# Seven products in the last dense chunk, and expert weight sums kept as plain sums

## The chip, the cores and the metric

The kernel runs on one core of a Trainium2 chip. The metric is the device time of one execution in microseconds; the times before are 1785.57, 1784.61 and 1784.65 us, median 1784.65.

PE is the matmul engine, PEld its weight load, DVE the vector engine, ACT the scalar engine, POOL the general one; SP issues transfers. A tile lies in SBUF (on-chip memory, 128 partitions) or in PSUM (the banks that PE writes to).

## The reference

All in float32. Attention with 32 packed rows, for 4 batches, 8 heads, 576 positions and head width 64:

```python
p_packed = sm_attn(p, k, v)
out = sm_attn(q, p_packed, p_packed)
```

Its result becomes x, of 2304 tokens by 512, and goes through a dense layer and a layer of 8 experts that every token visits:

```python
h = x @ w_in                       # w_in 512 x 2048
g = h * (1.0 / (1.0 + np.exp(-h)))
x = g @ w_out                      # w_out 2048 x 512

logits = x @ w_gate
P = np.exp(logits - logits.max())
for _ in range(8):
    P /= P.sum(1, keepdims=True) + 1e-09
    P /= P.sum(0, keepdims=True) + 1e-09
    P *= N / E
for e in range(E):
    h = np.maximum(x @ w1[e], 0.0)     # w1[e] 512 x 1024
    out += P[:, e:e + 1] * (h @ w2[e]) # w2[e] 1024 x 512
```

## The kernel before

Every float32 operand of a large product is kept as a sum of two halves, hi (ACT casts it to the reduced type float32r) and lo (DVE subtracts hi from the raw value; `split`, lines 145 and 146). A product is three matmuls: hi by hi, hi by lo, lo by hi.

**Dense layer.** The hidden columns go in four chunks c of 512. Attention gives, for each batch, a small matrix U (its packed values times w_in) from which the hidden values come by 24 matmuls of 128x288 for half a batch and half a chunk (`gemm1`, line 652). U is made as Uh (ACT, line 637) and Ul (DVE, line 638). ACT applies silu from PSUM (683) and casts the hi half (684), DVE subtracts for the lo half (685); both halves lie in `ring`. The second product (`gemm2_wide`, line 736) takes tiles of 384 tokens by 128 output columns: 12 matmuls each, with d counting the four blocks of 128 output columns, and a token tile holding two thirds of a batch. A chunk has 24 such tiles, 288 matmuls. In half of the tiles the old x2 (the output so far) is copied into the PSUM bank first (`seed`) and ACT copies the sum back (741); in the others DVE adds (743).

**What runs beside it.** Two trickles of work are fed in as the dense chunks run, each by a counter that the products advance (`pump`): `convs(c + 1)`, which turns the raw w_in and w_out of the next chunk into rounded halves (lines 528 to 546, tiles `win`, `ct`), at rate `CONV`; and `pre_w1`, at rate `RATE[c]`, which prepares expert weights. The instruction order on PE, DVE and ACT is the order of the code here (a manual schedule).

**Expert weights.** A step s is one expert and one half of its 1024 hidden columns, 16 steps, each run for three groups of tokens: a small group (256 tokens, steps 0 to 15, plain products) and two large ones (steps 16 to 47) in which a product of 2 x 2 blocks is made from seven block products in place of eight (numbers 1 to 7). For these, four sums of blocks of w1 are needed in each step (products 6, 7, 5, 3), the products 1, 2 and 4 use plain blocks. `pre_w1` makes the four sums for all 16 steps (line 851, tiles `S`), splits each into halves (`po`) and SP stores both halves in device memory (`w1d<-po`). In the large groups `w1_get` fetches hi and lo (512 KB) for the products with sums, and for the others loads the raw block of 256 KB (`rb`) and splits it. In the small group w1 and w2 are loaded again and split into whole halves (`w1l`, `w2l`, 128x1024).

## Time and profile before

| what | value |
|---|---|
| profiled execution | 1784.47 us, span 1782.7 us, granted clock 1.0 |
| PE busy | 1764.3 us, 99% |
| DVE busy | 1438.8 us, 81% |
| ACT busy | 1066.4 us, 60% |
| POOL busy | 1.0 us, 0% |
| DMA queue q1 | 340.14 MB, 54.7% of 16 engines |
| dense layer's second product, line 736, on the chain | 8% |
| dense layer's first product, line 652, on the chain | 5% |
| large groups, lines 1153 and 1201, on the chain | PE d 34%, X 20%, Z 10%, Y 5% |
| small group, lines 1046 and 1065, on the chain | u 5%, d 4% |

The span is the stretch from the first to the last instruction in the trace, the profiled execution's time is 1.8 us more. The shares on the chain say which line's work was the last to end at each moment. A duration in the trace holds the time that an instruction takes from start to end; neighbours on one engine overlap, so that the distance of two starts in a full queue is shorter than the duration.

### The profile page before, as it was taken

To read this page: it belongs to the slowest core of one execution; us is meant where nothing else is said; L and a number is where in the kernel's file an instruction comes from. 1 tells how busy PE (TensorE), PEld (TensorE's weight loads), DVE (VectorE), ACT (ScalarE), POOL (GpSimd) and SP (SyncE) were. 2 spreads that over 40 slices of the span, in tenths; PEclk is the share of its full clock that TensorE was granted. 3 is DMA by queue.
4 is the path that set the end of the run, shared out by engine and by line. 5 is a ranking of instruction groups with operands and counts; after the bars stand their busy time and mean duration, and the time that the engine had idled before them with its cause. 6 is when DMAs were issued, how large, how long until landed. Compare 5 with 4: busy or idle time off the path is not lost.

```text
span 1782.7 us, 25352 instructions
## 1 busy us (share of the span) xinstructions
PE 1764.3 (99%) x9564; PEld 1506.0 (84%) x9564; DVE 1438.8 (81%) x1918; ACT 1066.4 (60%) x1694; POOL 1.0 (0%) x8
## 2 busy tenths in 40 slices
PE   7999999999999999999999999999999999999998
PEld 4999999989998888888888888888888888888887
DVE  7868796759676988999889999887777777777778
ACT  6776675644454666665666666656555555555555
POOL 0000000000000000000000000000000000000000
PEclk9999999999999999999999999999999999999999
DMA  9326676875664655465544455964454444445432
GB/s 353 139 95 214 245 263 249 329 258 172 221 209 161 229 181 183 160 203 187 197 163 171 172 187 195 324 221 166 156 174 164 155 154 148 170 155 171 148 130 94
DMA packets 141498, 341.75 MB, mean 192 GB/s; under 512 B 11952, under 2 KB 49472, under 8 KB 140480
## 3 DMA queue, kind: packets, MB, share of 16 engines
q1 hardware_dynamic: 141376, 340.14, 54.7%
q8 instruction: 75, 1.23, 0.3%
q14 instruction: 47, 0.39, 0.1%
HBM read 256.66 MB, written 83.44 MB: 191 GB/s over the span
## 4 chain that ended last, share of the span: by engine, by line
PE 95%; DVE 2%; DMA 2%; ACT 1%; issue 0%; SPq 0%; DVEq 0%; ACTq 0%
PE d L1153 34%; PE X L1201 20%; PE Z L1201 10%; PE g2w L736 8%; PE g L652 5%; PE Y L1201 5%; PE u L1046 5%; PE d L1065 4%; PE g L704 3%; DMA v<-in_v_dram 1%; PE u L251 1%; DMA kq<-in_kT_dram 0%; PE pp L367 0%; PE s L251 0%; PE lg L1235 0%
## 5 line engine op out<-in xcount | busy, mean ns | idle before, releaser
L146 DVE TENSOR_TENSOR lo<-hb,hi 128x1024 fp32r<-128x1024 f32 x224 | 273.5, 1221 | 33.4 <-ACT hi L145 32.3
L1153 PE MATMUL d<-hi,w2f 128*128 128x512 f32 x896 | 294.2, 389 | 0.0
L1201 PE MATMUL X<-xf,w1l 128*128 128x512 f32 x1152 | 276.9, 389 | 0.0
L145 ACT CAST hi<-hb 128x1024 fp32r<-128x1024 f32 x224 | 235.4, 1052 | 64.9 <-PE d L1153 59.6
L1201 PEld LDWEIGHTS X<-xf,w1l 128*128 128x128 f32 x1152 | 216.2, 188 | 44.9
L1161 ACT COPY M<-d 128x512 f32<-128x512 f32 x234 | 137.4, 589 | 143.9 <-PE d L1153 140.7
L1165 DVE TENSOR_TENSOR M<-d,M 128x512 f32<-128x512 f32 x204 | 140.1, 687 | 100.8 <-PE d L1153 100.8
L1153 PEld LDWEIGHTS d<-hi,w2f 128*128 128x128 f32 x896 | 168.1, 188 | 34.9
L1153 PE MATMUL d<-lo,w2f 128*128 128x512 f32 x448 | 174.3, 389 | 0.0
L1153 PE MATMUL d<-hi,w2l 128*128 128x512 f32 x512 | 167.8, 389 | 0.0
L736 PE MATMUL g2w<-ring,woh 128*128 128x384 f32 x576 | 147.6, 337 | 0.0
L1149 ACT COPY d<-M 128x512 f32<-128x512 f32 x216 | 127.1, 589 | 21.1 <-DVE M L1165 19.7
L1153 PE MATMUL d<-hi,w2g 128*128 128x512 f32 x384 | 125.7, 389 | 0.0
L1153 PEld LDWEIGHTS d<-hi,w2l 128*128 128x128 f32 x512 | 96.1, 188 | 20.3 <-ACT d L1149 0.4
L736 PEld LDWEIGHTS g2w<-ring,woh 128*128 128x128 f32 x576 | 102.9, 188 | 8.6 <-issue 7.5
L1208 ACT COPY cp<-X 128x512 f32<-128x512 f32 x128 | 74.7, 583 | 47.2 <-PE X L1201 47.1
L1153 PE MATMUL d<-lo,w2l 128*128 128x512 f32 x256 | 99.6, 389 | 0.0
L1153 PEld LDWEIGHTS d<-lo,w2f 128*128 128x128 f32 x448 | 84.1, 188 | 17.5
L1201 PE MATMUL Y<-xf,w1f 128*128 128x512 f32 x384 | 97.3, 389 | 0.0
L736 PE MATMUL g2w<-ring,wol 128*128 128x384 f32 x288 | 96.3, 334 | 0.0
L1046 PE MATMUL u<-xs,w1h 128*128 128x256 f32 x512 | 94.4, 285 | 0.0
L145 ACT CAST w1f<-rb 128x512 fp32r<-128x512 f32 x96 | 59.8, 624 | 55.8 <-PE d L1153 41.0
(219 smaller groups left out, 3469.0 us busy)
## 6 DMA issues: line engine op xcount, KB each, us to landing
r<-in_moe_w_dram SPq DMA_DIRECT2D x128, 512.0 KB, 4.0
w1l<-w1d SPq DMA_DIRECT2D x128, 512.0 KB, 4.0
w1d<-po SPq DMA_DIRECT2D x64, 512.0 KB, 4.5
w2d<-w2f SPq DMA_DIRECT2D x64, 512.0 KB, 4.0
w2l<-w2d SPq DMA_DIRECT2D x64, 512.0 KB, 3.5
rb<-in_moe_w_dram SPq DMA_DIRECT2D x96, 256.0 KB, 2.6
sb<-in_moe_w_dram SPq DMA_DIRECT2D x48, 256.0 KB, 2.7
pb<-pd SPq DMA_DIRECT2D x16, 512.0 KB, 4.9
```

Of the source, the lines that this page charges most:

```text
L145: act.copy(out=hi, in_=raw)
L146: eng.tensor_tensor(out=lo, in0=raw, in1=hi.bitcast(F32), op=ALU.subtract)
L652: pe.matmul(ps, lhs[:, fs], rhs, start=(n == 0), stop=(n == 5))
L736: pe.matmul(ps[:, :TW], lhs[:, f % 2, ds], ring[f // 2][:, 2 * (f % 2) + rhs, q], start=(n == 0 and not on), stop=(n == 11), skip_group_ch ...
L1046: pe.matmul(ps[:, i], w[:, k % 2, f], x[:, k], start=(n == 0), stop=(n == 11))
L1065: pe.matmul(ps, h[:, l, f % 2, 128 * tt:128 * tt + 128], w[:, f % 2], start=(fh == 0 and n == 0), stop=(fh == 1 and n == 11))
L1149: act.copy(out=ps, in_=m)
L1153: pe.matmul(ps, w[:, l, c, 128 * d:128 * d + 128], r[:, c], start=(n == 0 and not seed), stop=(n == 5), skip_group_check=seed)
L1161: act.copy(out=m, in_=ps)
L1165: dve.tensor_tensor(m, ps, m, op=ALU.add)
L1201: pe.matmul(ps, w[:, l, c, 128 * i:128 * i + 128], x[:, r, c], start=(n == 0 and p in (1, 7)), stop=(n == 5), skip_group_check=p in (2, 6, ...
L1208: act.copy(out=t, in_=ps)
```

## The change

- In the last chunk (c = 3) the second product is made from seven block products: the hidden values as 2 x 2 blocks of 256 hidden columns and 288 tokens, w_out as 2 x 2 blocks of 256 by 256. The h-forms are differences of raw silu values (`minus`), split by ACT and DVE into `ft`; the weight forms `wS` are made from the converted raw w_out by four sums and seven splits (`w_forms`). The seven products of a batch accumulate in three pairs of PSUM banks, X (products 1, 6, 5, 3), Z (7, 4) and Y (2, which is seeded with x2); after each product DVE adds the bank's present value to one of the four x2 blocks, for Y ACT copies it. Each product is 2 blocks of output columns times 6 matmuls of 128x288.
- `pre_w1` writes the sums over their raw blocks, with two pairs of raw tiles (`r1`, `rx`), and POOL stores the two tiles of a step plainly (`keep_sums`); for the steps in `WHOLE` the sums are split and POOL stores hi and lo (`keep_form`). The steps in `LATER` get their sums in the small group, in the last two parts of the step before. The rates change; no such work is left in the last chunk.
- In the large groups a sum that is kept plain is loaded like a raw block (256 KB), ACT casts hi and writes minus hi into the lo half, and POOL issues a transfer that adds the stored sum to it. `rb` has three tiles for two and is loaded one part later.

The diff, cut to its core:

```diff
-RATE = {1: 36 / 64, 2: 36 / 64, 3: 41 / 53}
-CONV = 0.6
+RATE = {1: 23 / 64, 2: 23 / 64}
+CONV = {1: 0.6, 2: 0.8}
 TW = 384
 LATE = 3
 AHEAD = 3
+WHOLE = (0, 1, 15)
+LATER = (8, 10, 12, 14)
...
+            if c == NC - 1:
+                wz[j] = z.rearrange("p (k f) -> p k f", k=2)
+                return
...
+    SUM = {6: (0, 0), 7: (0, 1), 3: (1, 0), 5: (1, 1)}
+
+    def part(s, p):
+        j, h = SUM[p]
+        return raw1[s, j][:, :, 256 * h:256 * h + 256]
+
+    def sums_a(s):
+        dve.tensor_tensor(part(s, 5), part(s, 7), part(s, 5), op=ALU.add)
+        dve.tensor_tensor(part(s, 7), part(s, 6), part(s, 7), op=ALU.subtract)
+
+    def sums_b(s):
+        dve.tensor_tensor(part(s, 6), part(s, 5), part(s, 6), op=ALU.subtract)
+        dve.tensor_tensor(part(s, 3), part(s, 3), part(s, 6), op=ALU.subtract)
+
+    def keep_sums(s):
+        for j in range(2):
+            t = tc.dram_tile([128, 2, FH], F32, name=f"w1s{s}_{j}")
+            nc.gpsimd.dma_start(t, raw1[s, j])
+            for h in range(2):
+                w1d[s, {v: k for k, v in SUM.items()}[j, h]] = t[:, :, 256 * h:256 * h + 256]
+
+    def keep_form(s, p):
+        t = unit([128, 2, 2, 256], F32R, f"po{s}_{p}")
+        split(t[:, 0], t[:, 1], part(s, p))
+        nc.gpsimd.dma_start(dram(w1d, s, p), t.bitcast(F32))
+
+    def pre_w1(todo):
+
+        for i in range(2):
+            for j in range(2):
+                load_w1(todo[i], j, ("r1", "rx")[i])
+        yield
+        yield
+        later = None
+        for i, s in enumerate(todo):
+            sums_a(s)
+            if later:
+                load_w1(later[0], 0, later[1])
+                load_w1(later[0], 1, later[1])
+            yield
+            sums_b(s)
+            if s not in WHOLE:
+                keep_sums(s)
+            else:
+                for p in SUM:
+                    yield
+                    keep_form(s, p)
+            nxt = todo[i + 2] if i + 2 < len(todo) else 0 if i % 2 == 0 else None
+            later = None if nxt is None else (nxt, ("r1", "rx")[i % 2])
+            yield
+        if later:
+            load_w1(later[0], 0, later[1])
+            load_w1(later[0], 1, later[1])
 
...
         t = st[name].tile([128, 2, 256], F32, tag=name, name=f"rb{s}_{p}")
         r, c = 256 * (p != 1), FH * fh + 256 * (p == 4)
-        nc.sync.dma_start(t, w1[e, r:r + 256, c:c + 256].rearrange("(c p) f -> p c f", p=128))
+        nc.sync.dma_start(t, w1[e, r:r + 256, c:c + 256].rearrange("(c p) f -> p c f", p=128)
+                          if p in (1, 2, 4) else w1d[s % G0, p])
         raw1[s, p] = t
 
...
     def w1_get(s, p):
-        if p not in (1, 2, 4):
+        if s % G0 in WHOLE and p not in (1, 2, 4):
             wf[s, p] = get(w1d, s, p)
+            return
+        t = unit([128, 2, 2, 256], F32R, f"w1f{s}_{p}")
+        raw = raw1.pop((s, p))
+        if p in (1, 2, 4):
+            split(t[:, 0], t[:, 1], raw)
         else:
-            t = unit([128, 2, 2, 256], F32R, f"w1f{s}_{p}")
-            split(t[:, 0], t[:, 1], raw1.pop((s, p)))
-            wf[s, p] = t
+            act.copy(out=t[:, 0], in_=raw)
+            act.activation(t[:, 1], t[:, 0].bitcast(F32), AF.Copy, scale=-1.0)
+            nc.gpsimd.dma_start(t[:, 1], w1d[s % G0, p], accum_op=ALU.add)
+        wf[s, p] = t
 
     def w2_block(s, p):
...
-        for name, n in (("S", 4), ("r1", 2), ("po", 2)):
+        for name, n in (("S", 4), ("r1", 2), ("rx", 2)):
             open_(name, n, keep=name in ("S", "r1"))
-        box["pre"] = pre_w1(list(range(G0)), 0)
...
+    def w_forms():
+        while len(wz) < 2:
+            yield
...
+        ta, tb = (st["S"].tile([128, 2, 256], F32, tag="S", name=f"ws{n}") for n in "ab")
+
+        def form(p, x):
+            wS[p] = unit([128, 2, 2, 256], F32R, f"wS{p}")
+            split(wS[p][:, 0], wS[p][:, 1], x)
+
+        form(1, a11)
+        yield
+        dve.tensor_tensor(tb, a11, a21, op=ALU.subtract)
+        form(7, tb)
+        yield
+        dve.tensor_tensor(ta, a21, a22, op=ALU.add)
+        form(5, ta)
+        yield
...
+        yield
+
+    wf_ = w_forms()
...
+        def g_unit(k, j, half):
+            if k not in box["raw"]:
+                box["raw"][k] = dict(zip((11, 12, 21, 22, 5), raw_set(k)))
+            ps = box["pg"].tile([128, 2, 512], F32, tag="pg", name=f"g1_{k}{half}{j}")
+            for i in range(2):
+                gemm1_mm(ps[:, i, :HS], c, o[k], half, 2 * j + i)
+            act.activation(box["raw"][k][10 * (j + 1) + half + 1], ps[:, :, :HS], AF.Silu)
...
+        def h_form(k, p, x):
+            if "ft" not in box:
+                box["ft"] = hp.tile([128, 4, 2 * S], F32R, tag="h0", name="ft")
+            t = box["ft"][:, fn[0] % 4].rearrange("p (l c s) -> p l c s", l=2, c=2)
+            fn[0] += 1
+            split(t[:, 0], t[:, 1], x)
+            box["f"][k, p] = t
+
+        def minus(out_, a, b_):
+            dve.tensor_tensor(out_, a, b_, op=ALU.subtract)
+
+        def forms_a(k):
+            r = box["raw"][k]
+            h_form(k, 1, r[11])
+            minus(r[11], r[12], r[11])
+
+        def forms_b(k):
+            r = box["raw"][k]
+            minus(r[12], r[22], r[12])
+            h_form(k, 7, r[12])
+            minus(r[5], r[22], r[11])
+
+        def forms_c(k):
+            r = box["raw"][k]
+            h_form(k, 6, r[5])
+            minus(r[5], r[21], r[5])
...
+        CH = {1: "X", 6: "X", 5: "X", 3: "X", 7: "Z", 4: "Z", 2: "Y"}
+        OUT = {1: (0, 0), 6: (1, 0), 5: (1, 1), 3: (0, 1), 7: (1, 1), 4: (1, 0), 2: (0, 0)}
...
+        def seed2(k):
+            for d in range(2):
+                box["Y", d] = box["p3"].tile([128, 512], F32, tag="y", name=f"sY{k}{d}")
+                act.copy(out=box["Y", d][:, :HS], in_=acc_of(k, 2, d))
...
+        def product(k, p):
+            w, t, ch = wS[p], box["f"].pop((k, p)), CH[p]
+            for d in range(2):
+                if p in (1, 7):
+                    box[ch, d] = box["p3"].tile([128, 512], F32, tag="y", name=f"s{ch}{k}{d}")
+                ps = box[ch, d][:, :HS]
+                n = 0
+                for f in range(2):
+                    for l, r in ((0, 0), (0, 1), (1, 0)):
+                        pe.matmul(ps, w[:, l, f, 128 * d:128 * d + 128], t[:, r, f],
+                                  start=(n == 0 and p in (1, 7)), stop=(n == 5),
+                                  skip_group_check=p not in (1, 7))
+                        n += 1
+                dst = acc_of(k, p, d)
+                if p == 2:
+                    act.copy(out=dst, in_=ps)
+                else:
+                    dve.tensor_tensor(dst, ps, dst, op=ALU.add)
+            step()
...
+        need(4)
+        g_unit(0, 0, 0)
+        wide()
+        g_unit(0, 0, 1)
+        wide()
+        wide()
+        wide()
+        forms_a(0)
+        g_unit(0, 1, 1)
+        make_u(c, o[1])
+        forms_b(0)
+        g_unit(0, 1, 0)
+        for k in range(4):
+            r, more = box["raw"][k], k < 3
...
+            product(k, 1)
+            if k == 0:
+                forms_c(0)
+                need(5)
+                h_form(0, 4, r[5])
+            if more:
+                g_unit(k + 1, 0, 0)
+            h_form(k, 5, r[11])
+            product(k, 7)
+            h_form(k, 2, r[21])
+            need(6)
+            product(k, 6)
+            if more:
+                g_unit(k + 1, 0, 1)
+            h_form(k, 3, r[22])
+            need(7)
+            product(k, 4)
+            if more:
+                forms_a(k + 1)
+                g_unit(k + 1, 1, 1)
+            seed2(k)
+            product(k, 5)
+            if more:
+                forms_b(k + 1)
+                g_unit(k + 1, 1, 0)
+            if k < 2:
+                make_u(c, o[k + 2])
+            product(k, 2)
+            if k == 2:
+                cvn = pre0()
+            if more:
+                forms_c(k + 1)
+            product(k, 3)
+            if more:
+                h_form(k + 1, 4, box["raw"][k + 1][5])
+        for _ in cvn:
+            pass
...
-                q += 3
-                if q < 7 * NS and ORD[q % 7] in (1, 2, 4):
+                q += 2
+                if q < 7 * NS:
                     w1_block(q // 7, ORD[q % 7])
...
+                if s + 1 in LATER and slot >= 2:
+                    (sums_a, sums_b)[slot - 2](s + 1)
+                    if slot == 3:
+                        keep_sums(s + 1)
...
-        for name in ("acc", "r2", "gh", "po"):
...
+        for name in ("acc", "r2", "gh", "rx"):
             closers[name].close()
-        for name, n in (("hb", 6), ("hi", 3), ("lo", 3), ("rb", 2)):
+        for name, n in (("hb", 6), ("hi", 3), ("lo", 3), ("rb", 3)):
```

DVE at the place in chunk 2 where Ul of the third batch stands. `x2a` is the dense output, `po` and `S` the expert sums' halves and sums, `ring` the lo half of the hidden values, `ct` the raw w_out in conversion, `r` and `rx` raw expert blocks. Before:

```order
L743 TENSOR_TENSOR x2a_788<-g2w_2874,x2a_788 128x384
L146 TENSOR_TENSOR po_6_2891<-S_2_2832,po_6_2891 128x512
L685 TENSOR_TENSOR ring_103<-graw,ring_103 128x2x288
L531 TENSOR_SCALAR ct_2888<-ct_2888 128x1024
L532 TENSOR_SCALAR ct_2888<-ct_2888 128x1024
L146 TENSOR_TENSOR po_7_2915<-S_3_2849,po_7_2915 128x512
L685 TENSOR_TENSOR ring_1745<-graw,ring_1745 128x2x288
L534 SCALAR_TENSOR_TENSOR ct_2888<-rawout_2758,ct_2888 128x1024
L638 TENSOR_TENSOR Ul_2948<-u_2938,Uh_2947 128x1024
```


and after:

```order
L866 TENSOR_TENSOR r_71_2759<-r_70_2757,r_71_2759 128x2x256
L867 TENSOR_TENSOR r_70_2757<-r_70_2757 128x2x256
L748 TENSOR_TENSOR x2a_788<-g2w_2823,x2a_788 128x384
L533 TENSOR_SCALAR ct_2814<-ct_2814 128x1024
L534 TENSOR_SCALAR ct_2814<-ct_2814 128x1024
L870 TENSOR_TENSOR r_70_2757<-r_71_2759,r_70_2757 128x2x256
L871 TENSOR_TENSOR r_71_2759<-r_71_2759,r_70_2757 128x2x256
L690 TENSOR_TENSOR ring_103<-graw,ring_103 128x2x288
L536 SCALAR_TENSOR_TENSOR ct_2814<-rawout_2693,ct_2814 128x1024
L690 TENSOR_TENSOR ring_1747<-graw,ring_1747 128x2x288
L541 ISA ct_2814<-rawout_2693,ct_2814 128x2048
L643 TENSOR_TENSOR Ul_2891<-u_2881,Uh_2890 128x1024
```


Ul stands behind sums over raw blocks (lines 866 to 871) and three more conversion operations, in place of splits.

PE at the end of the dense layer, where the gate's logits `lg` follow (`g2w` is a bank of the second product, `woh` and `wol` the halves of w_out, `sX`, `sY`, `sZ` the banks of the seven products). Before:

```order
L736 MATMUL g2w_4379<-ring_1745,woh_3168 128x384 x2
L736 MATMUL g2w_4379<-ring_1745,wol_3169 128x384
L736 MATMUL g2w_4379<-ring_1745,woh_3168 128x384 x2
L736 MATMUL g2w_4379<-ring_1745,wol_3169 128x384
L1235 MATMUL lg_4402<-x2b_1369,wg 32x256 x3
L1235 MATMUL lg_4402<-x2b_1370,wg 32x256 x3
L1235 MATMUL lg_4402<-x2b_1371,wg 32x256 x3
```


and after, the last batch's seven products without the first two:

```order
L1542 MATMUL sX_4063<-ft,wS_3211 128x288 x6
L1542 MATMUL sX_4071<-ft,wS_3211 128x288 x6
L1542 MATMUL sZ_4085<-ft,wS_3480 128x288 x6
L1542 MATMUL sZ_4093<-ft,wS_3480 128x288 x6
L1542 MATMUL sX_4063<-ft,wS_3193 128x288 x6
L1542 MATMUL sX_4071<-ft,wS_3193 128x288 x6
L1542 MATMUL sY_4147<-ft,wS_3554 128x288 x6
L1542 MATMUL sY_4149<-ft,wS_3554 128x288 x6
L1542 MATMUL sX_4063<-ft,wS_3521 128x288 x6
L1542 MATMUL sX_4071<-ft,wS_3521 128x288 x6
L1267 MATMUL lg_4214<-x2b_1373,wg 32x256 x3
L1267 MATMUL lg_4214<-x2b_1374,wg 32x256 x3
```


Nothing of the first product lies between these, and each pair reads a form of `ft`.

ACT in a large group (`hb`, `hi` hidden values, `d` and `M` sums of products, `w1f` the halves of a w1 form, `w2f` those of w2). Before:

```order
L145 CAST xs_10402<-xr_9396 128x512
L145 CAST hi_2_10430<-hb_10177 128x1024
L145 CAST w1f_1_10427<-rb_1_10284 128x512
L1149 COPY d_10434<-M_6735 128x512
L1161 COPY M_6681<-d_10380 128x512
L145 CAST w2f_1_10451<-r_280_10208 128x512
L145 CAST w1f_2_10469<-rb_2_10332 128x512
L145 CAST hi_4_10473<-hb_10177 128x1024
```


and after:

```order
L948 CAST w1f_6_9842<-rb_6_9746 128x512
L949 ACTIVATE w1f_6_9842<-w1f_6_9842 128x512
L147 CAST w2f_7_9869<-S_3_9865 128x512
L1193 COPY M_6626<-d_9797 128x512
L1181 COPY d_9848<-M_6677 128x512
L948 CAST w1f_7_9898<-rb_7_9790 128x512
L147 CAST hi_3_9904<-hb_9731 128x1024
L949 ACTIVATE w1f_7_9898<-w1f_7_9898 128x512
L147 CAST w2f_5_9925<-S_1_9814 128x512
L1193 COPY M_6677<-d_9848 128x512
```


The rows of lines 948 and 949 are the hi half and minus hi of a sum, which ACT had no part in before.

## Rows read from the trace of the kernel before

**Rows 1.** The page: busy us, share of the span and instructions of each engine.

```profile
PE 1764.3 (99%) x9564; PEld 1506.0 (84%) x9564; DVE 1438.8 (81%) x1918; ACT 1066.4 (60%) x1694; POOL 1.0 (0%) x8
```

**Rows 2.** Chain that ended last, 340 to 376 us: start us, us, what.

```profile
...
345.95 8.32 PE g2w L736 x48
354.28 3.19 PE g L652 x24
...
369.96 4.44 PE lg L1235 x56
...
```

**Rows 3.** DVE's starts, 235.2 to 242.6 us: start, us, line, operation, out<-in.

```profile
235.49 0.55 DVE L743 TENSOR_TENSOR x2a<-g2w,x2a 128x384 f32<-128x384 f32 x1
235.96 0.68 DVE L146 TENSOR_TENSOR po<-S,po 128x512 fp32r<-128x512 f32 x1
236.55 0.75 DVE L685 TENSOR_TENSOR ring<-graw,ring 128x576 fp32r<-128x576 f32 x1
237.22 0.68 DVE L531 TENSOR_SCALAR ct<-ct 128x1024 f32<-128x1024 f32 x1
237.94 0.69 DVE L532 TENSOR_SCALAR ct<-ct 128x1024 uint32<-128x1024 uint32 x1
238.55 0.68 DVE L146 TENSOR_TENSOR po<-S,po 128x512 fp32r<-128x512 f32 x1
...
240.96 1.22 DVE L638 TENSOR_TENSOR Ul<-u,Uh 128x1024 fp32r<-128x1024 f32 x1
242.09 1.21 DVE L539 CUSTOM_DVE_ANT_0 ct<-rawout,ct 128x2048 uint16<-128x2048 uint16 x1
```

**Rows 4.** PE's starts from 241.9 us; in brackets the idle before and its releaser.

```profile
242.23 0.40 PE L652 MATMUL g<-a2h,Ul 128*128 128x288 f32 x1 [0.38 <-DVE Ul L638]
```

**Rows 5.** Lines by form, 131 to 400 us: count, busy us, mean ns, idle before.

```profile
L684 ACT CAST ring<-graw 128x576 fp32r<-128x576 f32 x48 | 32.4, 675 | 1.5
...
L637 ACT CAST Uh<-u 128x1024 fp32r<-128x1024 f32 x10 | 10.1, 1008 | 0.0
...
L741 ACT COPY x2a<-g2w 128x384 f32<-128x384 f32 x13 | 6.2, 480 | 11.5 <-PE g2w L736 11.4
```

**Rows 6.** Windows of chunk 1: length, busy us (instructions) of PE, PEld, DVE, ACT, POOL, ...

```profile
155.00:171.40 16.40, 16.24 (x113) 14.98 (x112) 14.11 (x21) 12.66 (x18) 0.00 (x0) 1.00 0.82 289
171.40:195.70 24.30, 24.30 (x164) 23.28 (x163) 23.30 (x34) 17.89 (x29) 0.00 (x0) 1.00 0.82 275
195.70:211.60 15.90, 15.90 (x113) 14.93 (x112) 10.13 (x16) 10.07 (x18) 0.00 (x0) 1.00 0.85 324
211.60:236.10 24.50, 24.50 (x161) 23.25 (x160) 20.55 (x30) 18.20 (x29) 0.00 (x0) 1.00 0.53 179
...
```

**Rows 7.** The page's DMA issues: count, KB each, median us from issue to landing.

```profile
r<-in_moe_w_dram SPq DMA_DIRECT2D x128, 512.0 KB, 4.0
...
w1d<-po SPq DMA_DIRECT2D x64, 512.0 KB, 4.5
...
rb<-in_moe_w_dram SPq DMA_DIRECT2D x96, 256.0 KB, 2.6
```

**Rows 8.** Windows of DVE alone, steps 7, 11 and 13 of the small group.

```profile
451.40:462.60 11.20, 6.41 (x9) 1.00 0.82 243
...
496.40:507.60 11.20, 9.16 (x12) 1.00 0.56 190
...
518.80:530.10 11.30, 8.49 (x10) 1.00 0.83 267
```

**Rows 9.** A weight block in a large group: ACT's cast, PE's first use, a window.

```profile
899.05 0.62 ACT L145 CAST w1f<-rb 128x512 fp32r<-128x512 f32 x1 [0.60 <-PE d L1153]
...
920.61 0.62 PE L1201 MATMUL X<-xf,w1f 128*128 128x512 f32 x2
...
640.00:1110.00 470.00, 470.00 (x2075) 389.19 (x2074) 423.80 (x566) 296.65 (x467) 0.00 (x0) 1.00 0.52 182
```

More of the change, by code (lines that the diff above doesn't have):

```diff
@@ L1389, in fused_kernel @@
                 gemm1(c, b, half, pump)
-                if half == 1 and nxt is not None and not first:
+                if half == 1 and not first:
                     if nxt[0] != c:
@@ L1396, in fused_kernel @@
                 keep = {0: 2, 1: 2, 2: 2, 3: 4}[unit_]
-                if (c, b) == seq[NC][:2]:
+                if first:
                     keep = len(tiles)
-                if nxt is None and half == 1:
-                    keep = 0
                 while len(tiles) > keep:
@@ L1403, in fused_kernel, with step @@
                     gemm2_wide(*n, tiles[1] if len(tiles) > 1 else None, pump)
-                    if n == (NC - 1, order[c][2] // 2, 0, 3):
-                        for _ in pre:
-                            pass
-                        cvn = Rot([pre0()], 1)
-        cvn.drain()
+        cv_st.close()
+        c, o = NC - 1, order[NC - 1]
+        cvn = iter(())
+        hr, hr_st = pool("hr", 1, side="right", reuse_waits="tile")
+        box["raw"], box["f"] = {}, {}
+        fn = [0]
+        def step():
+            next(cvn, None)
@@ new lines, in wide, with need @@
+        def wide():
+            n = tiles.pop(0)
+            gemm2_wide(*n, tiles[1] if len(tiles) > 1 else None, lambda w: None)
+        def need(n):
+            while len(wS) < n:
+                next(wf_)
+        need(4)
[12 more added lines that the diff above has]
+            r, more = box["raw"][k], k < 3
+            if k == 1:
+                hr_st.close()
+                a2b_st.close()
+                open_("gh", 6)
+                open_("r2", 2)
+                load_w2(0, 0)
+                load_w2(0, 1)
+            product(k, 1)
+            if k == 0:
+                forms_c(0)
[24 more added lines that the diff above has]
+            product(k, 2)
+            if k == 2:
+                cvn = pre0()
[4 more added lines that the diff above has]
+                h_form(k + 1, 4, box["raw"][k + 1][5])
```

92 lines of the change are left out of this document (42 added, 50 removed).

## The prediction

> **What bounds the kernel now.** I read the page's busy line first: PE is busy for 1764.3 us of a span of 1782.7, 99% [rows 1]. Then I read the chain that ended last, in the stretch of the last dense chunk: it is PE after PE with no other engine in it, and it carries the prices of its pieces: 48 matmuls of 384 columns take 8.32 us, 24 of 288 take 3.19, that is 0.1733 and 0.1329 us each [rows 2]. Third, the list of engine starts around the boundary of chunk 1 to chunk 2: VectorE (DVE) runs without a gap there, and its starts give the cost of an operation in a full queue (start to start, which is less than the duration printed): 0.47 for a 384-column addition from PSUM, 0.59 for 512 columns, 0.67 for 576, 0.61 for TENSOR_SCALAR on 1024, 1.13 for a tensor-tensor of 1024 [rows 3]. Just there PE waits, 0.38 us for DVE's Ul [rows 4]: the place shows how close DVE is to PE although its share is lower on average. So removed matmuls are worth their full time, removed DVE work is worth nothing by itself, and added or differently placed DVE work costs whatever comes out behind PE.
>
> **Part 1, the last chunk's second product.** 288 matmuls of 384 columns go and 336 of 288 come (7 products × 2 × 6 × 4 batches): 288 × 0.1733 − 336 × 0.1329 = 49.9 − 44.6 = −5.3 us, all on the path. What the form asks of the other engines: 28 splits of 576 columns in place of 16, the differences, 48 additions of 288 columns and 16 seeds and copies in place of 24 additions and 24 seeds and copies of 384. Three places can wait.
>
> *First batch.* Product 4 accumulates onto the banks that product 7 filled, so PE must wait until DVE has added product 7's value. From the last 384-column product on, DVE has to do before that: nine 576-column operations (9 × 0.67 = 6.0), one Ul (1.13), four additions of 288 columns (0.37 each, by columns from the 0.47: 1.5) and the low part of one weight form (0.6), 9.2 us [rows 3]. It starts about 1.0 late, since the first low part needs its cast on ScalarE (ACT; 0.68 [rows 5]); inside, it waits about 1.5 for Ul's cast (1.0 itself [rows 5], queued behind others) and about 1.4 for the casts of the other forms. Together 13.1 us. PE's own work up to product 4 is four g units of 12 matmuls and the products 1, 7 and 6 (12 matmuls of 288 columns each, 7 × 1.6 = 11.2) and the product for one U, 1.3 (what a 24.3 us window [rows 6] has left beside two pieces of 8.32 and two of 3.19): 12.5. So 0.6 is late. The next batch's product 1 takes the banks that Y leaves, through an ACT copy (0.48 for 384 columns [rows 5]) behind two queued casts: 0.8 more; and three smaller steps of the same chain at about 0.25, the other products' forms. I take 2.2, with bounds 0.5 (the copy alone) and 2.5. In the later batches PE has 18.9 us of work each (11 × 1.6 + 1.3) and DVE about 13, and no weight forms: they have room.
>
> *Last batch.* No first-product matmuls lie between the seven any more. DVE needs 13.5 us for that batch (six operations of 576, 4.0; twelve additions, 4.4; the four weight halves of MoE step 0 at 1.13, 4.5; and small parts of the gate's input, 0.6), PE 11.2 for the products and about 1 for the gate matmuls that don't need the last sums. 13.5 − 12.2 = 1.3, and about 0.4 from the last sum to the gate matmul that needs it: 1.7, bounds 0 (the weight halves could run later) and 2.1.
>
> **Part 2, sums over the raw blocks.** DVE drops 64 splits' low parts of 512, with 64 casts of ACT, and keeps the 64 sums (of which 16 move into the small group); 12 low parts remain for the three steps stored whole. But the work now ends inside chunks 1 and 2, not in chunk 3. Between Ul of chunk 2's second batch and that of its third, the order has 33 DVE rows for 32, with twelve 512-column operations for fourteen, three custom ones for two, six TENSOR_SCALAR for four: by the starts of [rows 3] 23.4 us for 22.2, in a PE time of 24.5 [rows 6]. The stretch before it grows from 9.6 to 10.8. So Ul stands 2.4 us later in DVE's queue; it was 0.38 late already [rows 4], but DVE has 24.5 − 20.55 = 4.0 of idle in the window before [rows 6], of which about 1.1 can be used (the rest is waiting for PE's own results). I take 1.3 more of PE waiting, bounds 0 (the idle takes all) and 2.4 (it takes none).
>
> Loads and stores: sums are now stored from the raw tiles themselves, so the load of the step after next waits for the store. Chunk 1 lasts 81.1 us (its four windows [rows 6]) and offers 23 pieces, 3.5 us each. A step's sums stand 3 pieces, 10.6 us, behind the store that frees their tile; the load's issue 1.2 later, the store 4.5 and the load 4.0 [rows 7] make 9.7, less than 10.6. The store is issued by POOL, which issues none before; the nearest row is SP's store of the same 512 KB, 4.5, and I take that. It is hidden up to 5.4. Low end: 2.6, the load of half the size; high end 8, twice the load of the same size [rows 7]. A load that waits for its tile holds SP's queue: behind it stand the next raw blocks of the expert weights and of the dense output weights, which are wanted a chunk later, so only the loop itself is at stake. On POOL nothing but stores is queued.
>
> The Trainium skill, "DMA: Bandwidth & Descriptors", section "Anatomy of one DMA — SWDGE (gpsimd) path", puts such a transfer at 2.0 us plus bytes/436e3. For 512 KB that is an estimate of 3.2 us, under the row's 4.5; no row of the trace before shows the path, and by that price the loop would be further from waiting and the sum the same.
>
> **Part 3, the small group.** The sums of steps 8, 10, 12 and 14 are four 512-column operations each, 2.4 us, made in the later half of steps 7, 9, 11 and 13. The fullest and the emptiest of those windows have 9.16 and 6.41 us of DVE work in 11.2 [rows 8]. 6.41 + 2.4 = 8.8 and 8.49 + 2.4 = 10.9 fit; 9.16 + 2.4 = 11.6 does not, by 0.4, and DVE can't use the 1 us that it stands there in handovers from ACT. I take 1.4, bounds 0 (lead of the weight halves covers it) and 2.6 (the three fuller steps by 0.9 each).
>
> **Part 4, the large groups.** 104 fetches of stored hi and lo become a load of 256 KB, two ACT operations and a POOL transfer that adds into the low half. PE gets the half later than before by the transfer. The cast of a block stands at 899.05 and PE's first use at 920.61, 21.6 us later [rows 9]; the second ACT operation ends about 2 us after the first began, so 15 to 19 us are left for the transfer, 11 at the change of group. The row nearest to it is the 256 KB load, 2.6 [rows 7]; twice that, for reading what is added to, is 5.2. I take 5.2 and cost it at nothing; low end 2.6, high end 12 (the lead at the change of group, nearly), still nothing. What waits behind it is only POOL's next transfer, four a step of 38 us. If the cover is gone, each microsecond beyond costs up to 104. ACT gains 104 × (0.6 + 0.6) = 125 us at most, over the two groups of some 570 us each; its share in the first goes from 296.65/470 = 63% to about 74% [rows 9], and PE waits on none of its queue there. Taken at nothing, with DVE unchanged.
>
> **Sum.** −5.3 + 2.2 + 1.7 + 1.3 + 1.4 = +1.3. The profiled execution took 1784.47 us, 1.8 above its span; the median of the runs is 1784.65. 1784.65 + 1.3 is about 1786.
>
> **The rivals.** *The queues keep up* (R1): DVE's lateness is swallowed by the idle that it has in every window, only 1 us of the four is paid. For it: the longest wait of PE in chunks 1 to 3 is the 0.38 us of [rows 4], and DVE is busy for 81% of the span only [rows 1]; against it: that wait is already one for DVE. −5.3 + 1.0 = −4.3: 1780.2. *The store paces the loop* (R2), the one on the slower side: if POOL's store takes more than 5.4 us, each of six links of the two-tile loop is late by the excess; at 8 us that is 6 × 2.6 = 15.6, less some 10 of DVE idle (5.8 and 4.0 in two windows of chunk 1 [rows 6]): 5 us on top, 1791. For it: this queue carries nothing before, so its price is unseen; against: 4.5 from the nearest row. *The accumulate is later than its lead* (R3): at 16 us or more PE waits in every step; 1 us each is 104: about 1890. Against: three times the dearest row of this size. *Descriptors held up by DVE* (R4): a store that has to wait until DVE leaves an operation of one kind starts at most one such operation late, 0.7 for the TENSOR_SCALAR of 1024 [rows 3]; 4.5 + 0.7 = 5.2, near the 5.4, so some links would be late by half a microsecond: 1788.
>
> The Trainium skill, "SBUF — State Buffer", section "Who interferes with whom", has the rule under R4: descriptors of transfers issued by GpSimd are written through a port that VectorE locks in its two-port modes. No transfer of that kind is in the trace before, so nothing here bears it out yet.
>
> **How the numbers follow.** Forecast 0.48 (its own range 1783 to 1788.2), R1 0.22, R2 0.18, R4 0.06, R3 0.04, the rest nothing. About 0.2%, 3.6 us, is what a measurement can tell from no change: faster means under 1781.1, slower over 1788.2. Faster is R1 for the most part, 0.20, and 0.02 of the forecast: 0.22. Slower is R2, R3, half of R4 and 0.03 of the forecast: 0.28. Same 0.50. The range: the low bounds of all four terms together are 0.5, 1780 less a little; the high ones 9.6, 1789; R2 lies at 1791, R3 is left out. 1780.5 to 1792.
>
> **What would show it.** In the profile after: 336 matmuls of 288 columns in place of 288 of 384, and no change elsewhere on PE. Waits of PE for Ul of chunk 2's first batches, for the h-forms and copies of the last chunk's first batch, for sums before the gate matmuls, and for the small group's halves in steps 9 to 13: each of about its term. POOL's store rows between 3 and 5.4 us; DVE waiting for raw blocks would be R2. In the large groups PE busy without a gap; waits there for the accumulated half would be R3, and would make the whole prediction wrong. If the four waits add up to under 2 us, R1 holds.

## The result: 10.7 us slower

The changed kernel took 1795.39 us (median of 4 runs, 1792.98 to 1796.17) against 1784.68 before: a ratio of 1.0057, 95% interval 1.0039 to 1.0074. The forecast was 1786, its range ended at 1792.

The profiled execution after has a span of 1793.2 us, 10.5 more than before. Busy time on the page, to set beside [rows 1], with the granted clock in 40 slices:

```profile
PE 1765.3 (98%) x9612; PEld 1504.2 (84%) x9612; DVE 1445.5 (81%) x1939; ACT 1149.7 (64%) x1859; POOL 136.5 (8%) x150
...
PEclk9999989999999999999999999999999999999999
```

PE is busy 1.0 us longer, though 5.3 us of its matmuls went; the clock row has an 8 for a 9 in the sixth slice, and that slice is where the largest loss is. PE's waits after (engine, line, tile, what it waited for: us, times, longest):

```profile
PE s L253 <- DMA kq<-in_kT_dram: 11.8, 2, 11.5
PE g L657 <- DVE Ul L643: 6.5, 1, 6.5
PE d L1097 <- DVE w2l L148: 1.9, 3, 0.8
...
PE sZ L1542 <- DVE x2b L1550: 0.5, 1, 0.5
...
PE sY L1542 <- ACT sY L1531: 0.3, 1, 0.3
```

The wait for Ul is [rows 4] grown from 0.38 to 6.5 us. DVE around it (start, us, instruction, in brackets the idle before and its releaser):

```profile
228.62 1.22 DVE L536 SCALAR_TENSOR_TENSOR win<-rawin,win 128x1024 uint32<-128x1024 uint32 x1
235.82 0.69 DVE L866 TENSOR_TENSOR rx<-rx,rx 128x512 f32<-128x512 f32 x1 [5.98 <-DMA rx<-in_moe_w_dram]
...
248.13 1.22 DVE L643 TENSOR_TENSOR Ul<-u,Uh 128x1024 fp32r<-128x1024 f32 x1
```

DVE stood for 6 us at a sum, since its raw block had not landed; the conversions, sums and Ul (248.13) are queued behind it. Then PE, at Ul's first use:

```profile
249.41 0.61 PE L657 MATMUL g<-a2h,Ul 128*128 128x288 f32 x1 [6.55 <-DVE Ul L643]
249.81 0.44 PE L657 MATMUL g<-a2h,Uh 128*128 128x288 f32 x1
250.05 0.44 PE L657 MATMUL g<-a2l,Uh 128*128 128x288 f32 x1
```

Starts are 0.24 us apart, for 0.133 in [rows 2]. In the table by stretch (length, busy us and instructions of PE, PEld, DVE, ACT, POOL, granted clock, DMA share, GB/s) the cause stands in the clock column:

```profile
222.00:236.00 14.00, 14.00 (x93) 14.00 (x92) 7.92 (x12) 8.13 (x13) 1.77 (x3) 1.00 0.98 331
236.00:249.40 13.40, 6.68 (x48) 5.12 (x46) 13.18 (x18) 5.80 (x8) 2.14 (x4) 0.84 0.85 291
249.40:255.00 5.60, 5.59 (x23) 5.59 (x24) 1.36 (x3) 1.33 (x2) 0.00 (x0) 0.50 0.99 334
255.00:262.50 7.50, 7.50 (x49) 7.35 (x47) 7.40 (x12) 3.52 (x6) 1.52 (x2) 0.98 0.65 227
```

PE was idle for half of 236 to 249.4. Within that stretch the granted clock fell to 0.50, that is 1.2 of 2.4 GHz, and it stayed there until about 255. PE's first 22 matmuls after the wait took 5.4 us where 22 times 0.133 is 2.9, so that with the start of the next product some 2.7 us were lost on top of the wait. The first row shows why the block was late: the DMA engines were 98% busy at 331 GB/s. What was under way, first POOL's stores, then SP's loads:

```profile
221.00 0.53 POOL L876 DMA_DIRECT2D w1s<-rx  x1 [11.05 <-DVE rx L870]
221.72 0.53 POOL L876 DMA_DIRECT2D w1s<-rx  x1 [0.19 <-issue]
225.72 0.53 POOL L876 DMA_DIRECT2D w1s<-r  x1 [3.46 <-DVE r L870]
226.44 0.99 POOL L876 DMA_DIRECT2D w1s<-r  x1 [0.19 <-issue]
```

```profile
222.99 0.37 SPq L520 DMA_DIRECT2D rawout<-in_moe_w_out_dram  x1
223.93 2.68 SPq L828 DMA_DIRECT2D rx<-in_moe_w_dram  x2
...
238.44 0.37 SPq L520 DMA_DIRECT2D rawout<-in_moe_w_out_dram  x1
```

These are stores of 1 MB at 221.0 and of 1 MB at 225.7, 1 MB of dense weights at 223.0, and between them the two tiles of the raw block that DVE waits for. The first is issued at 223.9, the second at 226.2, when its tile's store, issued at 221.7, had landed. The block was there at 235.8, 9.6 us after the second issue, where [rows 7] has 4.0.

By stretches, the 10.5 us are: 0.9 of a later first transfer (the first products start at 11.47 us instead of 10.53, in code that the change leaves alone; in the profiles of all runs here this start lies between 10.4 and 11.8), -0.4 in chunk 1, 9.3 at Ul with its half clock, -2.5 in the last chunk, 2.9 in the small group (187.4 us for 184.5) and 0.3 in the large ones.

### The profile page after: what moved, and what is told of

It reads as the page before. It is cut to its first block, busy times and chain, and to the rows that moved or that the text cites. A ratio compares the mean times of both kernels' runs of the same rounds, so it can differ in the third digit from the quotient of the medians.

```text
span 1793.2 us, 25825 instructions
## 1 busy us (share of the span) xinstructions
PE 1765.3 (98%) x9612; PEld 1504.2 (84%) x9612; DVE 1445.5 (81%) x1939; ACT 1149.7 (64%) x1859; POOL 136.5 (8%) x150
## 4 chain that ended last, share of the span: by engine, by line
PE 88%; DVE 5%; issue 3%; DMA 2%; ACT 1%; POOL 0%; SPq 0%; DVEq 0%; POOLq 0%; ACTq 0%
PE d L1185 33%; PE X L1233 19%; PE Z L1233 10%; PE Y L1233 5%; PE g L657 4%; PE u L1078 4%; PE d L1097 4%; PE g L709 3%; PE g2w L741 3%; PE sX L1542 1%; PE u L253 1%; DMA kq<-in_kT_dram 1%; DMA rx<-in_moe_w_dram 1%; PE sZ L1542 0%; PE s L253 0%
## 5 line engine op out<-in xcount | busy, mean ns | idle before, releaser
L1233 PE MATMUL X<-xf,w1f 128*128 128x512 f32 x1320 | 317.1, 389 | 0.0
L1233 PEld LDWEIGHTS X<-xf,w1f 128*128 128x128 f32 x1320 | 247.7, 188 | 51.4
L950 POOL DMA_DIRECT2D w1f<-w1s x104 | 114.1, 1097 | 1042.4 <-ACT w1f L949 519.6
L1233 PE MATMUL Z<-xf,w1f 128*128 128x512 f32 x696 | 167.3, 389 | 0.0
L1233 PEld LDWEIGHTS Z<-xf,w1f 128*128 128x128 f32 x696 | 130.6, 188 | 27.1
L741 PE MATMUL g2w<-ring,woh 128*128 128x384 f32 x384 | 98.7, 337 | 0.2 <-DVE x2a L748 0.2
```

Source lines behind the costliest of these rows:

```text
L741: pe.matmul(ps[:, :TW], lhs[:, f % 2, ds], ring[f // 2][:, 2 * (f % 2) + rhs, q], start=(n == 0 and not on), stop=(n == 11), skip_group_ch ...
L950: nc.gpsimd.dma_start(t[:, 1], w1d[s % G0, p], accum_op=ALU.add)
L1233: pe.matmul(ps, w[:, l, c, 128 * i:128 * i + 128], x[:, r, c], start=(n == 0 and p in (1, 7)), stop=(n == 5), skip_group_check=p in (2, 6, ...
```

## The experiments

All are edits of the changed kernel; e2 leaves out work that the result needs. Each ratio is to runs of the kernel before on the same chip, with medians from 1785.1 to 1785.8. The median of that kernel differs by up to 1.1 us from chip to chip (it was 1784.68 beside the changed kernel), so a smaller difference between edits on different chips says little.

**What delays the raw block.** e2 leaves out eight of the nine plain stores of the dense chunks (the large groups use step 2's sums instead).

```diff
     def keep_sums(s):
+        if s not in LATER + (2,):
+            for p in SUM:
+                w1d[s, p] = w1d[2, p]
+            return
```

> The eight plain stores of the dense chunks after the first one (steps 3 to 7, 9, 11, 13, 8 MB in all) are left out; the large groups use step 2's sums in their place. Theory A (the DMA engines are full where stores, raw blocks and raw dense weights meet): raw blocks land in about 4 us, DVE doesn't wait for them, PE's wait for Ul falls under 1 us and the half clock goes: about 1786. If the loads themselves (with the dense weights) fill the engines, part of the wait stays: 1790.

1787.21 us, ratio 1.0012 (1.0004 to 1.0021). The wait for Ul is 1.0 us and the clock stays whole. The same two stretches:

```profile
222.00:236.00 14.00, 14.00 (x93) 14.00 (x92) 13.79 (x20) 8.21 (x13) 0.00 (x0) 1.00 0.81 279
236.00:249.40 13.40, 12.36 (x87) 11.12 (x87) 13.23 (x20) 9.38 (x14) 0.00 (x0) 1.00 0.62 217
```

The second has 217 GB/s for 291, and PE 12.36 busy of 13.4 for 6.68. So stores and their consequences cost some 8 us. That doesn't yet say whether it is their bytes, their issuer, or that loads wait for them.

e3 has SP issue the stores (`nc.sync` for `nc.gpsimd` in `keep_sums` and `keep_form`).

> The same stores, issued by SP instead of POOL. Theory A (bytes, not the issuer): DVE still waits for raw blocks by several us and PE for Ul: 1792 to 1798, perhaps more since a store that waits for its sums now holds the loads behind it on SP. Theory B (POOL's issue path is slow or held up): the wait goes, about 1786.

1796.7 (1.0062; 1.005 to 1.0075), the wait for Ul is 8.6 us. So POOL as the issuer is not the cause.

e5 gives a plain step three pieces for two.

```diff
-RATE = {1: 23 / 64, 2: 23 / 64}
+RATE = {1: 26 / 64, 2: 26 / 64}
...
             if s not in WHOLE:
                 keep_sums(s)
+                yield
```

> Only the pace of the raw-block loop is changed: a step kept plain gets three pieces instead of two, at 26 pieces per 64 instead of 23, so that a step's 2 MB of load and store come every 9.4 us instead of every 7 us; the same operations and bytes otherwise. Theory A (2 MB in 7 us is 300 GB/s, about all that the DMA engines moved there, and dense weights come on top): the raw blocks land in time and PE's wait for Ul falls to about 1 us, without a stretch at half clock: 1795.4 - 8.5 = about 1787, near the kernel without the stores (1787.2). Rival (DVE's own work ahead of Ul is too much, stores or not): the wait stays at several us, 1792 or more.

1787.7 (1.0017; 1.0008 to 1.0026): the same bytes in a longer time take away 7.7 us. They don't in every run: eleven runs went from 1786.39 to 1792.93, and in the profiled one (1790.83) DVE still waited once for a block, and PE 2.0 us for Ul.

```profile
DVE r L866 <- DMA r<-in_moe_w_dram: 2.7, 1, 2.7
```

t3 keeps pace and bytes and gives the loop a third place for raw blocks (the tiles of pool `S`, idle then, in four quarters of 256 KB), so that a load needs the store of three steps ago.

```diff
+        names = ("r1", "rx", "S")
...
-            nxt = todo[i + 2] if i + 2 < len(todo) else 0 if i % 2 == 0 else None
-            later = None if nxt is None else (nxt, ("r1", "rx")[i % 2])
+            nxt = todo[i + 3] if i + 3 < len(todo) else 0 if i % 3 == 0 else None
+            later = None if nxt is None else (nxt, names[i % 3])
```

> A third place for raw blocks in the dense chunks (the four tiles of pool S, loaded and stored in quarters of 256 KB), so that a load has one step more of lead; the pace of 23 pieces per 64, the bytes and all else as in the changed kernel. Theory A' (each load lands late because it must wait for a store and then shares the DMA engines, and the lead of a step covers a burst): PE's wait for Ul falls from 6.5 us to 1 or less and the half clock goes: 1786 to 1787. Rival (the DMA engines can't move the bytes in that stretch at all): the burst comes later but the wait stays at 4 us or more, 1792.

1787.24 (1.0011; 1.0002 to 1.002), as without stores. Its stretches, and PE's waits:

```profile
222.00:236.00 14.00, 14.00 (x93) 14.00 (x93) 13.79 (x21) 7.91 (x13) 3.03 (x6) 1.00 0.85 298
236.00:249.40 13.40, 12.45 (x88) 11.21 (x87) 10.24 (x15) 7.00 (x11) 3.33 (x6) 1.00 1.00 369
```

```profile
PE d L1117 <- DVE w2l L148: 2.4, 4, 0.8
PE g L657 <- DVE Ul L643: 0.9, 1, 0.9
```

DMA is fuller than in the changed kernel (369 GB/s and 100% in the second), and PE waits 0.9 us. So it isn't that the engines can't move the bytes: the loop of two tiles had no lead over a burst. (One step in three is also moved in smaller transfers there; no run has the third place without that.)

**Sums on POOL.** e1 has `nc.gpsimd.tensor_tensor` for all sums over raw blocks.

> The sums over the raw blocks are made by POOL instead of DVE, in the dense chunks and in the small group; all else as in the changed kernel. Theory A (the sums stand in DVE's queue ahead of Ul and wait there for raw blocks that land 9.5 us after their issue; PE then runs at the half clock for a while): the loads land as late as before, but Ul no longer stands behind them, so PE's wait of 6.5 us and the stretch at half clock (about 2.7 us lost) go, and the three waits for w2l in the small group (1.9 to 2.4 us) go too: 1795.4 - 9.2 - 2.2 = about 1784. Theory B (the queue of POOL is what makes the raw-block loop late): the loop gets slower still, since POOL now also adds, and what needs its end waits: 1795 or more. A price for a POOL addition of 512 columns isn't in any trace yet; if it is 3 us or more, four of them and the store no longer fit the loop and the later steps' sums end after chunk 2.

1815.73 (1.0173; 1.0159 to 1.0187). The waits for Ul and nearly all for w2l are gone, as theory A had it, and a new one of 21.3 us came. On SP, then on DVE:

```profile
249.32 1.63 SPq L828 DMA_DIRECT2D rx<-in_moe_w_dram  x2
251.04 0.42 SPq L520 DMA_DIRECT2D rawout<-in_moe_w_out_dram  x1
```

```profile
259.89 1.35 DVE L533 TENSOR_SCALAR ct<-ct 128x1024 f32<-128x1024 f32 x1 [22.34 <-ACT ct L530]
```

The dense weights' load (`rawout`) stands in SP's queue behind raw blocks that wait for POOL's slower loop, and is issued at 251.04, in the changed kernel at 222.99. DVE and ACT stand at its conversion for 22 us, and with them what is queued behind it, so that PE waits too. And DVE itself ran longer beside POOL's additions. POOL's price by line, then DVE's for the lo halves and for one conversion (mean ns of one, 180 to 300 us):

```profile
L871 POOL TENSOR_TENSOR rx<-rx,rx 128x512 f32<-128x512 f32 x5 | 8.5, 1692 | 0.4
```

```profile
L690 DVE TENSOR_TENSOR ring<-graw,ring 128x576 fp32r<-128x576 f32 x18 | 17.1, 952 | 18.8 <-ACT ring L689 18.8
...
L536 DVE SCALAR_TENSOR_TENSOR ct<-rawout,ct 128x1024 uint32<-128x1024 uint32 x3 | 4.7, 1580 | 0.0
```

The lo halves took 952 ns, for 0.75 us in [rows 3], and the other operation 1580. The Trainium skill, "SBUF — State Buffer", section "Who interferes with whom", has a rule for it: a VectorE instruction with two inputs in SBUF and a GpSimd instruction that reads SBUF wait for each other at a shared port. The rows agree, with a mean of 27% more for the lo halves. They show more than this rule covers: the two TENSOR_SCALAR operations on `ct`, with one input each, took 1.27 and 1.37 us in the mean, for 0.69 in the changed kernel.

**The last chunk.** e4 makes the second product as before, with the 24 tiles of 384 tokens, all else as changed.

> The last chunk's second product is made as before (24 tiles of 384 tokens), all else as in the changed kernel. In the two traces the stretch from the start of chunk 3 to the gate is 2.5 us shorter with the seven products, so this should be 2.5 us above the changed kernel: 1798, with the same wait for Ul in chunk 2. By the prediction's own terms (-5.3 + 2.2 + 1.7) it would be 1.4 above, 1796.8. If ACT and DVE had been held up by the forms far into the gate, it would be below 1795.

1799.61 (1.0083; 1.0069 to 1.0097), 4.2 above the changed kernel, where 2.5 was expected. The profiled run is the slowest of the four, 1802.82. In it the way from the third U of chunk 2 (290.1 us) to the gate (383.0) takes 92.9 us, as before, so that the products' own worth stays 2.5. Ahead of that stretch stands a second wait, of 2.4 us for an ACT copy behind the late Ul, after which some 1.6 us are lost at half clock. That this wait is also what the medians have beyond 2.5 is not shown, since only this one run was profiled.

e7 moves the last three weight forms into chunk 2 (`while len(wS) < 7`).

> Only the last three weight forms of the seven products (for products 4, 3 and 2) are moved from the first batch of chunk 3 into the end of chunk 2. If DVE's queue in the first batch is what product 4 waits for: the waits there (0.2 + 0.7 us) go, about 0.9 off, 1794.5, wait for Ul in chunk 2 unchanged. If product 4 waits for ACT and the forms of h: no change.

1795.15 (1.005; 1.0037 to 1.0064). Runs of either kernel differ by over 3 us, so the times can't tell 0.9 from nothing; the trace can: the wait before product 4 is the same 0.69. DVE's queue there has a step that ACT holds up, as the chain of the changed kernel shows (start, us, what):

```profile
314.50 0.65 ACT rawt L1490
315.14 0.57 ACT ft L147
...
315.74 0.76 DVE ft L148
316.50 0.38 DVE x2b L1550
...
317.01 1.83 PE sZ L1542 x12
```

ACT's silu of the next batch goes ahead of a cast, whose lo half goes ahead of the sum that frees Z. f2 makes that form (product 5's) after the sum and swaps the last batch's products 2 and 3, on top of f1 below; f4 has the form alone; f3 adds to f2 that w1's halves for step 0 are made a batch earlier.

```diff
+            product(k, 7)
             h_form(k, 5, r[11])
-            product(k, 7)
```

> As f1, and in the last chunk the form for product 5 is made after product 7's sums are added, and the last batch does product 3 before product 2. If DVE's queue ahead of those sums and the seed of Y are what PE waits for there (0.7 and 0.5 us in the changed kernel's trace): about 1.0 less than f1, 1783 to 1784. If the order of DVE's queue doesn't matter there: no change to f1.

> As f1 (third place for raw blocks, slower pace, small group's sums on POOL) with the form for product 5 made after product 7's sums, without the swap of products 3 and 2 that cost 1.8 us in f2. Theory: f1's wait of 0.7 before product 4 falls to 0.45 and the swap's wait is gone: 0.3 below f1, about 1783.6. If f1 and this agree within 0.5, the order of that one form doesn't matter.

> As f2, and the halves of MoE step 0's w1 are made during the third batch of the last chunk, where DVE is idle for 5 us of 18.9, instead of in the last batch. If DVE's queue in the last batch is the wait there: 0.3 to 0.6 less than f2. If the halves have to wait for weight forms still in use: DVE stands in the third batch and it is 1 or more slower than f2.

f1 1783.9, f4 1783.66, f2 1786.2, f3 1788.1. The form's order gives some 0.3 us in the trace, too little for the times to tell: the wait of 0.69 before product 4 is gone, and one of 0.44 before product 5, for ACT's cast, came. The swap costs more than the 0.5 it was to save, since product 3 adds onto the bank that product 5's sum is still read from:

```profile
PE sX L1563 <- DVE x2a L1571: 1.8, 1, 1.8
```

f3 is slower than f2 by 1.9, as the second case of its expectation had it, but not for the reason given there. In its trace no half waits for a buffer: the halves' casts on ACT (1.05 us each) and their lo parts on DVE stand ahead of a form, DVE waits 0.7 us for one of the casts, and PE waits 2.2 us for a sum queued behind them, with 3.4 us at half clock.

**The small group.** e6 moves only its sums to POOL; e8 also slows the pace (24 per 64), takes steps 4 and 6 into the small group and makes the weight forms early.

> Only the four sums of the small group (steps 8, 10, 12, 14) are made by POOL instead of DVE; the dense chunks as in the changed kernel. With all sums on POOL the small group took 185.3 us, with DVE 187.4 (184.5 before), so: 2.1 us less, about 1793.3, the wait for Ul in chunk 2 unchanged. Rival (the small group's loss is DMA, not DVE's queue): no change, 1795.4.

> The slower pace (24 pieces per 64, three a plain step), two more steps (4 and 6) moved to the small group, its sums on POOL, and the weight forms made early, all together. By the terms: 1784.7 - 5.3 for the products, + 1.9 left of their waits after the early forms, + 0.8 to 1.2 for the small group, + 0.5 to 1 for Ul: 1783 to 1784, a little below the kernel before. If POOL's additions in the small group hold DVE up by the port (DVE ran 20 to 60% longer beside POOL's additions in the dense chunks), the two added steps cost another 1 to 2: 1785.

e6: 1793.45 (1.0044), 1.9 less. e8: 1792.51 (1.0043), far above the expected 1784: with two tiles the wait for Ul was still 4.8 us, and the two added steps cost two waits of 1.7 and 1.6 us in the small group. Single profiles of the small group have to be read with care: with its code as in the changed kernel it took 187.4 us there, and 187.8, 188.3, 189.3 and 189.5 in e2, t3, e5 and e7. f1 is the third place, the pace of e5 and the small group's sums on POOL.

> Third place, the slower pace (three pieces a plain step, 26 per 64) and the small group's sums on POOL. Theory A': the wait for Ul at about 0.5 to 1 in every run, the small group at 2 less: 1784 to 1785. If POOL's sums cost DVE time by slowing it, 1786.

1783.9 (0.9993; 0.9984 to 1.0002), no wait for Ul. But the small group still took 186.9 us. f5 puts steps 8 and 10 back into the dense chunks (`LATER = (12, 14)`), f6 all (`LATER = ()`).

> As f4, with the sums of steps 8 and 10 made in the dense chunks, and only 12 and 14 left to the small group; 29 pieces per 64. Open: whether the small group's 2.4 us over the kernel before are the four steps' sums and stores. If they are: half of it comes back, 1.2 below f4, about 1782.4, as long as the dense loop has room with the third place. If the dense loop is full: a wait for Ul of 2 us or more, 1785 or above.

> As f4, with all sums in the dense chunks, none in the small group; 33 pieces per 64. If the small group's 2.4 us are its sums: it takes 184.5 us as before, 2.4 below f4, 1781.2, unless the dense loop now waits. 26 MB of plain loads and stores, 9 MB of the whole steps and 8 MB of dense weights in some 150 us are 290 GB/s, near the 340 that the fullest stretches show: likely a wait for Ul or at the weight forms, 1786 or more.

1784.58 and 1784.63. In f6 the small group took 184.8 us, in f5 186.6: taking out steps 8 and 10 gave nothing there, and f6 pays for the rest in the dense chunks (1.6 us for Ul, and 0.6 for a U where f4 has no wait). What stays in f4 and f5 is the same row in both:

```profile
PE d L1118 <- DVE w2l L148: 1.4, 3, 0.8
```

f7 (`LATER = (8, 10, 14)`, 28 per 64) takes out step 12 alone; f8 is f7 with the small group's sums on DVE.

> As f4, with only step 12's sums (made in step 11 of the small group, whose window was DVE's fullest) put back into the dense chunks; 28 pieces per 64. In f4 and in f5 the waits of 0.4, 0.3 and 1.0 us stand in the same place, just where step 12's sums are made, whether steps 8 and 10 are there or not. Theory: the small group's excess is that one step's; the small group takes 184.6 to 185 us instead of 186.5, and the kernel is 1.7 below f4, about 1782. Rival (any sums cost about 0.5 each): 0.5 below f4.

> As f7, with the small group's three steps of sums (8, 10, 14) on DVE, as in the changed kernel. In the changed kernel's trace the waits for w2l were 0.67, 1.03 and 0.3 about step 12's sums and 0.3 above the usual one after step 14's; without step 12: 0.3 to 0.7 above f7, 1782.5. If DVE's queue recovers less well than that: 1783.5.

f7 1783.39 (0.9987; 0.9978 to 0.9996) and f8 1783.24 (0.999; 0.9981 to 0.9999): both just under the kernel before, with intervals that end below 1, though 0.1% is less than the 0.2% that the prediction took as the least one can tell. The small group takes 184.5 us in both, as before. PE's waits in f8:

```profile
PE g L657 <- DVE Ul L643: 1.1, 2, 0.7
...
PE d L1118 <- DVE w2l L148: 0.4, 1, 0.4
```

So the small group's loss in f4 is the one step whose window was the fullest, 9.16 us in [rows 8]; the three others cost nothing without it, on either engine. With all four on DVE, e5 and e7 have a further wait of 1.6 us after step 14's sums, which the changed kernel's profile doesn't have. In the times f7 is 0.3 below f4 and not the expected 1.7: in the two profiles the way from chunk 1 to the gate is 1.5 us longer in f7, through its waits for Ul and U, and the small group 2.0 shorter.

## Why the prediction was wrong

**The failed step: "the load's issue 1.2 later, the store 4.5 and the load 4.0 [rows 7] make 9.7, less than 10.6".** The store was right: the plain ones landed in 4.1 to 4.4 in the median, the one that frees the late tile in 4.5, and SP's do no better (3.7 and 4.9 in e3). Wrong were the load and the 10.6. The load took 9.6 us in the place that matters, with the engines 98% busy, and the sum had put it at a median. The page of after gives

```profile
r<-in_moe_w_dram SPq DMA_DIRECT2D x92, 512.0 KB, 4.3
...
rb<-w1s SPq DMA_DIRECT2D x104, 256.0 KB, 3.1
w1f<-w1s POOLq DMA_DIRECT2D x104, 256.0 KB, 5.1
...
rx<-in_moe_w_dram SPq DMA_DIRECT2D x28, 512.0 KB, 5.6
```

with 5.6 for `rx`, and even that median hides the worst link. And the 3.5 us per piece were a mean over chunk 1. From the first store's issue at 221.0 to the next sum's turn at 229.8, when DVE's operation before it ended, there were 8.8 us, not 10.6. From the second store's issue at 221.7 it is 8.1, in which 4.5 of store and 9.6 of load had to fit: 6.0 too much, which is DVE's wait of 5.98. Two pieces a plain step mean 2 MB of load and store in some 7 us, 300 GB/s, and 1 MB of dense weights every 15.4 us (223.0, 238.4) adds 68: more than the 331 GB/s that went through from 222 to 236 us. The working never added up the bytes. t3 and e5 show the two ways out: lead, or pace.

R2 named the loop and its sign, DVE waiting for raw blocks, but had the store as the slow part, and took off some 10 us of DVE's idle in two windows. No idle softened it: DVE's 5.98 came through to PE as 6.55. R2 gave 1791 with a chance of 0.18.

**A term that was missing: the clock.** After the wait of 6.5 us PE ran at half the clock for some 5.5 us, 2.7 us lost. The clock row of before has a 9 in all 40 slices, and the prediction priced a stall at its own length.

```profile
PEclk9999999999999999999999999999999999999999
```

**What stands in chunk 2 without the burst** is 0.9 to 1.0 us of wait for Ul (e2, t3), that is 0.5 to 0.6 more than the 0.38 of [rows 4], where the prediction had 1.3 more: inside its bounds, and less than half of it. With the slower pace as well (f1, f4) there is none.

**The last chunk: right mechanism, terms too large.** From the third U of chunk 2 to the gate, before and after:

```profile
277.04 1.02 PE u L251 x16
```

```profile
286.85 1.02 PE u L253 x16
```

The gate starts at 369.96 [rows 2] and, in the chain after, at 377.27:

```profile
373.36 0.41 ACT sY L1531
...
373.81 1.86 PE sY L1542 x12
...
377.27 4.44 PE lg L1267 x56
```

92.9 became 90.4, so -2.5 for the forecast -1.4. The waits are where they were put: before product 4 (0.7; forecast 0.6) and in the last batch about 1 us, half of it before the product on Y (forecast 1.7). With the -5.3 that makes -3.6; the other 1.1 is spread over the products' starts in small pieces that no run here takes apart. The wait of 0.8 for the copy of Y and the three smaller steps didn't come as waits of their own.

**The small group: 2.9 for 1.4**, above the bound of 2.6. That the window of 9.16 us doesn't fit and the others do was right; that the excess of 0.4 and 1 us of handover is what it costs was too little. PE waits for lo halves in both of the steps that follow, 11 us apart:

```profile
520.07 0.50 PE L1097 MATMUL d<-w2l,h 128*128 128x512 f32 x1 [0.51 <-DVE w2l L148]
...
531.09 0.50 PE L1097 MATMUL d<-w2l,h 128*128 128x512 f32 x1 [0.76 <-DVE w2l L148]
```

By the distances of the starts these are 0.67 and 1.03 us, with a further 0.3 at 532.9 and 0.3 more than before near the group's end: 2.3 of the 2.9. The rest was not traced.

**The large groups: as forecast.** The accumulate landed in 5.1 us (forecast 5.2; the third of the DMA rows above), and PE never waits for it. That the number fits is partly luck: it was twice the plain load of [rows 7], 2.6, and that load itself took 3.1 here. ACT's share in the first group went to the 74% that was worked out:

```profile
650.00:1120.00 470.00, 470.00 (x2075) 389.15 (x2074) 423.01 (x565) 347.90 (x565) 52.62 (x48) 1.00 0.63 181
```

347.90 of 470 us, PE busy throughout, as in [rows 9]. R3 is out. R4 is out too: e3 has no transfers of that kind in the dense chunks and waits as long. R1 was wrong in the changed kernel; f7 and f8, with the third place, get 1.9 and 2.1 of the 4.3 us that it gave.

## What to carry to other kernels

Add up the bytes of a burst, by the engines' rate in a full row of the trace, before adding up durations: a median landing time (4.0 us here) says little about a load in a burst (9.6). A wait put into an in-order queue is paid by whatever stands behind it, so give such a loop one buffer more before making its work shorter. And when a wait of PE grows to several microseconds, price the clock that follows it, too.

## What the runs showed of the hardware

PE's waits for Ul of 6.5, 6.7 and 8.6 us (changed kernel, e6, e3) went with 10.2 us at a granted clock of 0.50, part of it while PE still waited; waits of 6.5 and 6.6 us at the same place in e7 and e4 went with 6.8 us, so that waits of one length can cost differently. One of 4.8 us (e8) went with 6.8, and waits of 2.0 (e5), 2.2 (f3) and 2.4 us (e4's second) with 3.4 us each. In e5 the clock fell 1.2 us after PE was back at work. Waits of 0.4 to 1.2 us for Ul (f5, f8, t3, e2, f6) and one of 1.8 in the last chunk (f2) went with none. POOL's addition of 512 columns takes 1.3 to 1.8 us in the means by line (e1), against 0.68 on DVE. A POOL transfer that adds into SBUF took 5.1 us for 256 KB, against 3.1 for the plain load of the same data. A stretch of 13.4 us moved 369 GB/s, loads and stores together (t3).
